# A later planned landing for the second chunk's queries and keys, and the clock-holding tile filled first

## The chip, the cores and the metric

The kernel runs on one core of a Trainium2 chip. The metric is the device time of one execution in microseconds (us), and lower is better. Ratios below 1 mean that a kernel is faster than the kernel before. A difference counts as faster or slower from 2%; below that it is "the same", although the repeated runs here resolve about 0.2%.

## The reference

```python
# q, k, v: [4, 8, 768, 64]
scores = q @ k.T / sqrt(64)
keep = causal                                    # heads 0, 2, 6
keep = causal & (first 4 keys | last 64 keys)    # the other heads
a = softmax(where(keep, scores, -1e9)) @ v
x = a.transpose(0, 2, 1, 3).reshape(3072, 512)   # tokens x (head, dim)
g, val = x @ w_gate, x @ w_val                   # d_ff = 1536
out = x + sigmoid(x @ w_res) * ((gelu(g) * val) @ w_out)
```

All inputs and the output are float32; the kernel computes in fp16 and accumulates in float32.

## The kernel before

The 3072 tokens are worked off in six chunks of 512. The kernel is written as a list of tasks. Each has an engine, a planned duration, a priority and the tasks that it depends on. A list scheduler runs when the program is built, and fixes the order of instructions on each engine; semaphores are then derived from the dependencies. So a planned duration or a planned landing changes nothing on the chip by itself. It changes the order, and an engine then waits in that order for whatever really comes late.

```python
# in the scheduler: when a load is planned to have landed
if t.dma:
    ...
    t.end = dma_free[e] + 1.6 + t.late
...
# the task g0 is the first gate matmul: with it the "warm" matmuls end
if t.name == "g0" and warming:
    warming = False
    cand["pe"] = [w for w in cand["pe"] if w.name != "warm"]
...
t_blank = G.add("dve", 0.1, lambda e: e.memset(blank[:, :], 0.0), [], -99, name="blank")
t_ident = G.add("dve", 0.1, lambda e: e.memset(ident[:, :], 0.0), [], -98, name="ident")
t_ident = G.add("pool", 0.3, aff(ident[:, :], ALU.not_equal, 1.0, ...), [t_ident], -58.5, name="const")
...                                        # m_causal, m_win: on GpSimd as well
# in loads_rows (chunks 0 and 1): queries and keys by rows, in halves for chunk 0
for j, src in enumerate((q, k)):
    t = dma("pool", base + 4 * gi + j, (h1 - h0) * n * 0.089, ..., bufs=[st])
...                                        # transposed on TensorE against ident (L676)
# fillers for TensorE, at the lowest priority
for _ in range(360):
    G.add("pe", 0.06, lambda e, warm=warm: e.matmul(at(warm)[:, 0:128], lhsT=blank[:, :], rhs=blank[:, :], ...),
          [t_blank], 1e9, bufs=[warm], name="warm")
load_weights()      # gate and value weights in three parts each, in turn: gate 1, value 1, gate 2, ...
```

GpSimd issues all loads of the inputs, which convert float32 to fp16, and it makes the identity (`ident`) and the masks in between. The warm matmuls are meant to hold TensorE's clock up until real work fills it. The string HINTS holds hand-found priorities of some hundred tasks, as "number of the task: priority".

The softmax here doesn't subtract the row's maximum and nothing guards it: scores larger than these inputs give would overflow.

Of the kernel before, what the change touches and what calls it, by code (L numbers as in the profile page):

```python
# [43 lines left out]


HINTS = (
    "0:598.78 2:-98.96 3:-24.27 16:511.03 398:-226.32 399:-81.95 400:-169.98 401:-133.18 406:592.76 "
    "428:669.65 590:-107.97 595:554.03 604:-62.97 609:119.02 611:508 631:-103.87 632:500.02 635:591.25 "
    "640:113.91 642:197.51 643:485.34 648:497.6 649:608.77 687:-2618.72 693:998.98 695:-156.54 696:-101.5 "
    "699:-194.37 703:460.62 704:468.99 706:91.16 707:1.21 708:-184.02 711:-2906.86 712:108.67 715:-113.61 "  # L50
    "722:-93.98 726:593.8 732:539.67 737:-3080.99 740:2426.17 743:-43.63 744:44.98 750:-84.74 755:-61.77 "
    "756:-226.32 757:-68.07 758:-100.39 762:-75.67 767:1467.66 783:2538.51 789:1088.69 791:2362.89 "
    "794:489.79 834:-1953.13 885:2499.66 897:2409.44 903:1361.62 910:1573 915:1075.62 921:1094.44 "
    "927:1527.46 933:2646.2 934:3345.41 946:3583 960:3450.9 963:1467.39 982:1981.84 984:1548.12 1014:3374.09 "
    "1025:2486.39 1037:3491.83 1060:2046.57 1061:2453.27 1067:3409.97 1068:1990.02 1069:3494.45 1076:2552.54 "
    "1081:2446.96 1082:3477.51 1099:2162.67 1105:3505.94 1111:3490.47 1117:3067.67 1144:3026.33 1146:3134.85 "
    "1150:118.46 1155:3543.75 1198:3516.67 1304:980.83 1313:4066.75 1341:4517.9 1343:4508.61 1358:985.12 "
    "1363:4003.98 1364:4417.91 1375:5441.35 1388:4117.01 1418:5399.99 1424:4517.89 1429:3494.32 1435:5479.84 "
    "1436:5423.25 1563:5565.33 1567:6542.91 1598:5535.71 1608:2079.98 1609:4991.07 1610:5503.31 1622:2043.57 "
    "1623:5529.25 1628:5543.06 1629:5543.02 1635:6420.01 1659:7430.01 1672:7417.77 1684:7455.84 "  # L60
)

class Task:
# [380 lines left out]
def c_mm(n, k=1):  # L444
    return k * max(0.029, n / 2400 + 0.0025)


def c_act(n):
    return 0.19 + n * 0.000834


def c_dve(n, rate=1.0, psum=True):
    return (0.125 if psum else 0.065) + n * 0.00104 / rate
# [6 lines left out]
def build_kernel(nc, q, k, v, w_gate, w_val, w_out, w_res, out):  # L460
    assert N_SINK <= 64 and WINDOW == 64
    G = Graph(nc)
# [16 lines left out]
    P_vk = Pool(many("vk", 2, [128, 8, DHEAD + 1], FP16))  # L479
# [21 lines left out]
    def at(buf):  # L501
        if buf.pool is P_ps:
            return psum[:, buf.slot[0] * 512:(buf.slot[-1] + 1) * 512]
        return buf.pool.items[buf.slot]

    def at16(buf):
        return at(buf).bitcast(FP16)
# [17 lines left out]
    t_blank = G.add("dve", 0.1, lambda e: e.memset(blank[:, :], 0.0), [], -99, name="blank")  # L525
# [17 lines left out]
    t_win = t_win0 + [spread(("dve",), 600, m_win[:, 5:7, :], m_win[:, 1:2, :].to_broadcast([128, 2, 128]), 256, t_win),  # L543
                      spread(("dve",), 600, m_win[:, 0, :], m_win[:, 1, :], 128, t_win)]
    for i, vk in enumerate(P_vk.items):
        P_vk.last[i] = [G.add("dve", 0.3, (lambda vk=vk: lambda e: e.memset(vk[:, :, :], 0.0))(), [], -94, name="vzero")]
    for i, va in enumerate(P_v.items):
        P_v.last[i] = [G.add("dve", 0.15, (lambda va=va: lambda e: e.memset(va[:, :, :, DHEAD:DHEAD + 1], 1.0))(),
                             [], -95, name="vones")]

    def dma(eng, prio, cost, out_ap, in_ap, bufs=(), deps=(), name="ld", grp=None):
        issue = 0.85 if eng == "pool" else 1.2
        return G.add(eng, issue, lambda e: e.dma_start(out_ap(), in_ap), deps, prio, bufs=bufs, dma=cost, name=name, grp=grp)  # L553
# [24 lines left out]
    def batch(b):  # L578
        if b not in batches:
            B_ = B()  # L580
            B_.v, B_.vs, B_.vk, B_.qkt = Buf(P_v), Buf(P_vs), Buf(P_vk), Buf(P_qkt)
            B_.vtok, B_.vstok, B_.qtok, B_.ktok = {}, {}, {}, {}

            B_.q6, B_.q6tok = None, {}
            batches[b] = B_
        return batches[b]
# [59 lines left out]
    def loads_rows(c, si, b, a, z):  # L646

        n = z - a
        BB = batch(b)
        st = Buf(P_st)  # L650
        lo, hi = a * 128, z * 128
        base = {0: -60, 1: -15, 2: 50}[c]
        groups = ((0, 4), (4, 8)) if c == 0 else ((0, 8),)
        tok = {}

        def sv(j, h0, h1, w):
            return at(st)[:, :].rearrange("p (j h w) -> p j h w", j=2, h=NHEAD)[:, j, h0:h1, 0:w]
        for gi, (h0, h1) in enumerate(groups):
            for j, src in enumerate((q, k)):
                t = dma("pool", base + 4 * gi + j, (h1 - h0) * n * 0.089,  # L660
                        (lambda j=j, h0=h0, h1=h1: lambda: sv(j, h0, h1, n * 64))(),
                        src[b, h0:h1, lo:hi, :].rearrange("h (p j) d -> p h (j d)", j=n), bufs=[st])
                for h in range(h0, h1):
                    tok[j, h] = t
        values(b, a, z, base + (10 if c == 0 else 2), False, c == 0)

        per = 1 if c == 0 or n == 4 else 2
        for k_ in range(0, NPAIR, per):
            ps_ = ORDER[k_:k_ + per]
            pr = 1000 * c - 492 + ps_[0] if c else 40 * k_ - 205  # L670
            for js in (((1,), (0,)) if c == 0 else ((0, 1),)):
                scr = Buf(P_ps, "scr" if c else "scr0")
                items = [(p, jj) for jj in js for p in ps_]

                def tr(e, items=items, scr=scr):
                    return [e.transpose(out=at16(scr)[64 * x:64 * x + 64, (m * n + i) * 128:(m * n + i + 1) * 128],  # L676
                                        in_=at(st)[:, (jj * NHEAD + h) * 256 + i * 64:(jj * NHEAD + h) * 256 + (i + 1) * 64],
                                        identity=ident[:, :])
                            for m, (p, jj) in enumerate(items) for i in range(n) for x, h in enumerate(PAIRS[p])]
                tt = G.add("pe", c_mm(128, n) * len(items), tr, [t_ident] + [tok[jj, h] for p, jj in items for h in PAIRS[p]],  # L680
                           pr, bufs=[st, scr], name="qkT")
                tt.mode = "col"


                def ev(on, p0=ps_[0], scr=scr, j0=js[0], m=len(items)):
                    def fn(e):
                        o = at(BB.qkt)[:, :, :, lo:hi].rearrange("c j (y x) w -> c x (j y) w", x=2)[:, p0 % 2]
                        m0 = j0 * 2 + p0 // 2
                        o = o[:, m0:m0 + m, :].rearrange("c m (p j) -> c m p j", j=n)
                        i_ = at16(scr)[:, 0:m * n * 128].rearrange("c (m j p) -> c m p j", m=m, j=n)  # L690
                        return e.tensor_copy(out=o, in_=i_) if on == "dve" else e.activation(out=o, in_=i_, func=AF.Copy)
                    return fn
                w = n * 128 * len(items)
                t = G.flex({"dve": (c_dve(w), ev("dve")), "act": (c_act(w), ev("act"))}, [tt], pr,
                           bufs=[scr, BB.qkt], name="qkE")
                for p, jj in items:
                    for i in range(a, z):
                        (BB.ktok if jj else BB.qtok)[p, i] = t
# [525 lines left out]
def bass_duo_attention_split__then__geglu_gated_residual_kernel(  # L1224
    nc: bass.Bass,
    q: bass.AP,
    k: bass.AP,
    v: bass.AP,
    is_retrieval: bass.AP,
    n_sink: bass.AP,  # L1230
    window: bass.AP,
    moe_w_gate: bass.AP,
    moe_w_val: bass.AP,
    moe_w_out: bass.AP,
    moe_w_res: bass.AP,
    out: bass.AP,
):
    assert int(n_sink) == N_SINK and int(window) == WINDOW
    build_kernel(nc, q, k, v, moe_w_gate, moe_w_val, moe_w_out, moe_w_res, out)
# [33 lines left out]
```

## Time and profile before

| | before |
|---|---|
| time, three runs | 272.18 us median, 271.61 to 272.54 |
| profiled execution | 272.37 us, of which the profile's span is 270.6 |
| idle TensorE ahead of the first warm matmul | 2.63 us |
| idle TensorE ahead of the second chunk's transposes | 0.53 us |
| TensorE after 36.78 us | without a gap, to 267.66 us |
| after the last matmul | 2.9 us (270.6 less 267.66) |

The prediction below shows the lines on which this rests. Three more views of the kernel before are needed. The first is GpSimd's timeline: start and duration in us, engine, line, operation.

```profile
1.32 0.88 POOL L553 DMA_DIRECT2D qks<-in_q_dram  x1 [0.81 <-DVE ident L526]
2.29 0.30 POOL L511 TENSOR_SCALAR_AFFINE_SELECT ident<-ident 128x128 f16<-128x128 f16 x1
2.53 0.77 POOL L553 DMA_DIRECT2D qks<-in_k_dram  x1
```

GpSimd issues the first q load, makes the identity, and only then issues the first k load. The second view is the list of DMA issues for the first 4 us: tile, queue, count, KB of each, us from issue to landing.

```profile
qks<-in_k_dram POOLq DMA_DIRECT2D x1, 256.0 KB, 5.4
```

Issued at 2.53, that k load landed at 7.93. The third view is TensorE's timeline, where the first q and then the first k transposes are.

```profile
6.05 1.06 PE L676 MATMUL ps<-ident,qks 128*64 128x128 f16 x16
...
7.99 0.64 PE L676 MATMUL ps<-ident,qks 128*64 128x128 f16 x16
```

The k transposes start right after the k load has landed.

### The profile page before, as it was taken

Reading aid. Unit: us, or ns where it says so; the run is one execution under the profiler, and the core shown is the slowest. Engines: PE = TensorE matmul, PEld = TensorE weight load, DVE = VectorE, ACT = ScalarE, POOL = GpSimd, SP = SyncE. Lnnn points to the kernel's source line nnn. Section 1 sums busy time; section 2 is a strip of 40 time slices with the busy share of each in tenths; the row PEclk is TensorE's granted clock in tenths of the full one; section 3 lists DMA queues with packets and bytes.
Section 4 is the critical chain, followed back from the end, with each engine's and each line's share of the span. In section 5 each row is a group of like instructions: output and inputs, shape, how many; then the busy total and the mean of one; then the engine's idle time right before and its main releaser. Section 6 shows DMA issues by size and latency. Waiting matters only on the chain.

```text
span 270.6 us, 5686 instructions
## 1 busy us (share of the span) xinstructions
PE 264.4 (98%) x2392; PEld 139.0 (51%) x2392; DVE 141.3 (52%) x275; ACT 139.6 (52%) x215; POOL 87.0 (32%) x124
## 2 busy tenths in 40 slices
PE   6999999999999999999999999999999999999995
PEld 5778554465444456444455444455444455444444
DVE  1798236387444466534477533376444377434344
ACT  2785456864245877233784233776323778043300
POOL 8999409995743037993000000000000000000000
PEclk9999999999999999999999999999999999999999
DMA  6999999999999999999964100013100014100013
GB/s 82 172 203 207 185 179 229 170 160 172 176 183 151 154 126 221 183 174 162 174 125 119 39 0 0 2 41 85 74 0 0 0 41 80 61 20 0 0 39 119
DMA packets 96506, 29.12 MB, mean 108 GB/s; under 512 B 84448, under 2 KB 92896, under 8 KB 96480
## 3 DMA queue, kind: packets, MB, share of 16 engines
q0 software_dynamic: 70320, 14.69, 64.3%
q1 hardware_dynamic: 26160, 14.07, 27.9%
q8 instruction: 19, 0.31, 0.5%
q14 instruction: 7, 0.06, 0.1%
HBM read 29.36 MB, written 6.29 MB: 132 GB/s over the span
## 4 chain that ended last, share of the span: by engine, by line
PE 85%; DMA 7%; POOL 6%; issue 1%; DVE 1%; POOLq 0%; DVEq 0%
PE ps L1111 41%; PE ps L1156 23%; PE ps L1141 8%; DMA qks<-in_k_dram 7%; PE ps L852 4%; PE ps L986 3%; POOL qks L553 2%; PE ps L976 2%; PE ps L1000 1%; PE ps L1065 1%; POOL va L553 1%; POOL wv L553 1%; PE ps L676 1%; PE ps L943 1%; POOL wg L553 1%
## 5 line engine op out<-in xcount | busy, mean ns | idle before, releaser
L1123 ACT ACTIVATE gact<-ps 128x512 f16<-128x512 f32 x68 | 40.2, 597 | 73.3 <-PE ps L1111 71.9
L1125 DVE SCALAR_TENSOR_TENSOR hT<-gact,ps 128x512 f16<-128x512 f16 x68 | 45.7, 687 | 61.7 <-ACT gact L1123 34.0
L1111 PE MATMUL ps<-xT,wv 128*128 128x512 f16 x272 | 74.6, 379 | 0.0
L1111 PE MATMUL ps<-xT,wg 128*128 128x512 f16 x272 | 74.1, 379 | 0.0
L1156 PE MATMUL ps<-wo,hT 128*128 128x512 f16 (+2 forms) x312 | 70.7, 363 | 0.0
L1111 PEld LDWEIGHTS ps<-xT,wv 128*128 128x128 f16 x272 | 26.3, 98 | 31.3 <-DMA wv<-in_moe_w_val_dram 0.4
L1111 PEld LDWEIGHTS ps<-xT,wg 128*128 128x128 f16 x272 | 26.3, 98 | 30.5 <-ACT xT L1072 0.6
L1156 PEld LDWEIGHTS ps<-wo,hT 128*128 128x128 f16 x312 | 27.2, 98 | 26.2 <-issue 1.0
L553 POOL DMA_DIRECT2D qks<-in_k_dram x36 | 28.6, 834 | 32.9 <-DMA qkt<-qks 22.5
L868 ACT ACTIVATE er<-ps 128x1024 f16<-128x1024 f32 (+4 forms) x40 | 34.2, 890 | 7.9 <-PE ps L852 7.6
L553 POOL DMA_DIRECT2D qks<-in_q_dram x36 | 28.8, 846 | 0.8 <-DVE ident L526 0.8
L1160 DVE SCALAR_TENSOR_TENSOR otile<-srs,ps 128x512 f32<-128x512 f32 (+2 forms) x26 | 16.8, 644 | 17.4 <-PE ps L1156 17.2
L1141 PE MATMUL ps<-wr,xT 128*128 128x512 f16 x96 | 24.5, 380 | 0.0
L553 POOL DMA_DIRECT2D va<-in_v_dram x24 | 21.5, 944 | 3.0 <-PE ps L1000 3.0
L1144 ACT ACTIVATE srs<-ps 128x512 f32<-128x512 f32 x24 | 14.3, 597 | 13.6 <-PE ps L1141 13.6
L852 PE MATMUL ps<-qkt 64*128 64x64 f16 (+3 forms) x391 | 17.2, 213 | 0.1
L1163 DVE TENSOR_TENSOR otile<-otile,xtok 128x512 f32<-128x512 f32 (+2 forms) x26 | 16.8, 647 | 0.7
L1043 DVE TENSOR_TENSOR xtok<-ps,rcp 128x512 f32<-128x512 f32 (+1 forms) x28 | 16.9, 609 | 0.5
L852 PEld LDWEIGHTS ps<-qkt 64*128 64x128 f16 x391 | 9.9, 94 | 9.3 <-issue 4.9
L868 ACT ACTIVATE es<-ps 128x1024 f16<-128x1024 f32 (+1 forms) x14 | 12.6, 900 | 3.0 <-PE ps L852 3.0
L1141 PEld LDWEIGHTS ps<-wr,xT 128*128 128x128 f16 x96 | 8.5, 98 | 9.5 <-issue 0.6
L1173 PE MATMUL ps<-blank 128*128 128x128 f16 x109 | 10.8, 248 | 2.6 <-DVE blank L525 2.6
(69 smaller groups left out, 216.1 us busy)
## 6 DMA issues: line engine op xcount, KB each, us to landing
out_dram<-otile SPq DMA_DIRECT2D x23, 256.0 KB, 2.0
va<-in_v_dram POOLq DMA_DIRECT2D x24, 128.0 KB, 18.5
qks<-in_k_dram POOLq DMA_DIRECT2D x32, 64.0 KB, 12.4
qks<-in_q_dram POOLq DMA_DIRECT2D x32, 64.0 KB, 13.0
wg<-in_moe_w_gate_dram POOLq DMA_DIRECT2D x3, 512.0 KB, 11.5
wv<-in_moe_w_val_dram POOLq DMA_DIRECT2D x3, 512.0 KB, 11.9
wo<-in_moe_w_out_dram POOLq DMA_DIRECT2D x4, 384.0 KB, 23.7
vs<-va SPq DMA_DIRECT2D x4, 260.0 KB, 6.7
```

The costliest lines, as they stand in the source:

```text
L553: return G.add(eng, issue, lambda e: e.dma_start(out_ap(), in_ap), deps, prio, bufs=bufs, dma=cost, name=name, grp=grp)
L852: return [e.matmul(at(scr)[:, oo:oo + w], lhsT=side(BB, low, 1)[half, k0:k0 + 128], rhs=side(BB, low, 0)[half, qq:qq + w], start=True, sto ...
L868: return e.activation(out=o, in_=i_, func=AF.Exp, scale=SM_SCALE)
L1043: t2 = G.add("dve", c_dve(2 * n * 64), lambda e: e.tensor_tensor(out=xview(), in0=avv(0, DHEAD), in1=scale(), op=ALU.mult), [t1] + xdeps, ...
L1111: return lambda e: [e.matmul(at(dst)[:, :], lhsT=w[:, ci, f * 128:(f + 1) * 128], rhs=at(xtbuf)[:, ci, :], start=(ci == 0), stop=(ci == NC ...
L1123: ta = G.add("act", c_act(512), (lambda gb=gb, ga=ga: lambda e: e.activation(out=at(ga)[:, :], in_=at(gb)[:, :], func=AF.Gelu))(), [tg], p ...
L1125: th = G.add("dve", c_dve(512), (lambda vb=vb, ga=ga, f=f: lambda e: e.scalar_tensor_tensor(out=at(h)[:, f, :], in0=at(ga)[:, :], scalar=0 ...
L1141: e.matmul(at(rb)[:, :], lhsT=at(xtbuf)[:, ci, s], rhs=wr[:, ci, :], start=(ci == 0), stop=(ci == NCB - 1))
L1144: ta = G.add("act", c_act(512), (lambda rb=rb, sr=sr: lambda e: e.activation(out=at(sr)[:, :], in_=at(rb)[:, :], func=AF.Tanh, scale=0.5)) ...
L1156: e.matmul(at(fb)[:, w], lhsT=at(h)[:, fi, s], rhs=wo[:, fi, w], start=(fi == 0), stop=(fi == NF - 1))
L1160: t1 = G.add("dve", c_dve(n), (lambda fb=fb, sr=sr, ot=ot, w=w: lambda e: e.scalar_tensor_tensor(out=at(ot)[:, w], in0=at(sr)[:, w], scala ...
L1163: t2 = G.add("dve", c_dve(n), (lambda ot=ot, lt=lt, w=w: lambda e: e.tensor_tensor(out=at(ot)[:, w], in0=at(ot)[:, w], in1=at(xbuf)[:, lt, ...
```

## The change

The intent has two parts. The loads of the second chunk's queries and keys are planned to land 1.2 us later, nearer to when they do land, so that the scheduler puts other work ahead of their transposes. And the other fills on VectorE are made to depend on the blank tile, so that it is filled first and the clock-holding matmuls start sooner. The hints were searched anew for this plan.

```diff
 HINTS = (
-    "0:598.78 2:-98.96 3:-24.27 16:511.03 398:-226.32 399:-81.95 400:-169.98 401:-133.18 406:592.76 "
     (13 more lines removed)
+    "1:-142.02 3:-32.5 13:-14.98 398:-205.14 399:-3161.01 400:-242.48 401:-60.67 406:194.11 430:523.84 "
     (12 more lines added)
 )
@@
     for i, vk in enumerate(P_vk.items):
-        P_vk.last[i] = [G.add("dve", 0.3, (lambda vk=vk: lambda e: e.memset(vk[:, :, :], 0.0))(), [], -94, name="vzero")]
+        P_vk.last[i] = [G.add("dve", 0.5, (lambda vk=vk: lambda e: e.memset(vk[:, :, :], 0.0))(), [t_blank], -94, name="vzero")]
     for i, va in enumerate(P_v.items):
         P_v.last[i] = [G.add("dve", 0.15, (lambda va=va: lambda e: e.memset(va[:, :, :, DHEAD:DHEAD + 1], 1.0))(),
-                             [], -95, name="vones")]
+                             [t_blank], -95, name="vones")]
@@ in loads_rows
                         src[b, h0:h1, lo:hi, :].rearrange("h (p j) d -> p h (j d)", j=n), bufs=[st])
+                t.late = 1.2 if c else 0.0
                 for h in range(h0, h1):
                     tok[j, h] = t
```

Task 2 is the making of the identity on GpSimd. Its hint of -98.96 is gone, which is how the first k load came ahead of it.

## The prediction

> **What bounds the kernel now.** I read the page first, for the busy shares and the chain that ended last.
>
> ```profile
> PE 264.4 (98%) x2392; PEld 139.0 (51%) x2392; DVE 141.3 (52%) x275; ACT 139.6 (52%) x215; POOL 87.0 (32%) x124
> ...
> PE 85%; DMA 7%; POOL 6%; issue 1%; DVE 1%; POOLq 0%; DVEq 0%
> ```
>
> TensorE is busy 98% of the span and carries 85% of the chain. DMA and GpSimd carry 13%, so I asked for the chain in order of time, to see where those 13% lie.
>
> ```profile
> 15.33 0.74 POOL wv L553
> 16.07 2.56 POOL qks L553 x3
> 18.63 18.01 DMA qks<-in_k_dram
> 36.64 0.14 issue
> 36.78 0.64 PE ps L676 x16
> 37.42 1.83 PE ps L1111 x8
> ```
>
> All of it comes before 36.78 us: GpSimd issues loads one behind the other, and the last of the second chunk's queries and keys, issued at 18.63, lands 18.01 us later. From there on the chain is TensorE alone, until the output's tail. The timeline of TensorE has only two idle stretches that it names in the whole run:
>
> ```profile
> 2.63 3.49 PE L1173 MATMUL ps<-blank 128*128 128x128 f16 x31 [2.63 <-DVE blank L525]
> ...
> 36.78 0.64 PE L676 MATMUL ps<-ident,qks 128*64 128x128 f16 x16 [0.53 <-DMA qks<-in_k_dram]
> ```
>
> The numbers are start, duration and, in brackets, the idle time before. The first is the wait of the clock-holding ("warm") matmuls for their blank tile, the second the wait of the second chunk's transposes for that load. Asking for three stretches confirms it (columns: stretch, its length, busy time, clock, DMA share, GB/s):
>
> ```profile
> 20.60:36.25 15.65, 15.64 (x133) 1.00 1.61 190
> 36.25:36.78 0.53, 0.00 (x1) 1.00 2.43 155
> 36.78:266.40 229.62, 229.62 (x1923) 1.00 0.86 98
> ```
>
> From the first gate/value matmul (20.60) to the last matmul, 0.53 us are idle out of 245.8. After that come 4.2 us of last evictions and output.
>
> **What the Trainium skill says.** "TensorE: Matmul & The Clock Gate", section "What's actually happening", has the array at half clock until it has been busy for about 3.4 us, and says that this varies from run to run. The trace agrees roughly: the 31 first warm matmuls take 3.4 us from 2.63 (110 ns each), those at 8.56 take 0.73 us for ten. The same page, "Back-to-back issue gap", puts a warm 512-column matmul at 512/2.4 + 2.5 = 216 ns; here a pair takes 0.43 us (35.21 to 35.65). "DMA: Bandwidth & Descriptors", "Issuing engines are not separate DMA queues", says that all loads share the same 16 engines. The trace agrees: with up to about 190 GB/s flowing, later issues take longer and longer from issue to landing (4.3 us for the first q load, 18.0 us for the load above).
>
> **The change, part by part.** The real work is untouched. The counts of every TensorE instruction but the warm ones are the same in both orders; warm ones go from 109 to 116, all ahead of the first gate/value matmul. What the diff changes are the planned landing, the priorities and two fills on VectorE, and hence the order on every engine.
>
> *The blank tile.* VectorE now runs ident, blank, then the four other fills. Before, blank came last:
>
> ```profile
> 0.89 0.11 DVE L526 MEMSET ident<- 128x64 uint32 x1 [0.89 <-PEq L1255]
> 1.12 0.10 DVE L548 MEMSET va<- 128x48 f16 x1
> 1.25 1.04 DVE L546 MEMSET vk<- 128x520 f16 x2
> 2.42 0.10 DVE L548 MEMSET va<- 128x48 f16 x1
> 2.46 0.11 DVE L525 MEMSET blank<- 128x64 uint32 x1
> ```
>
> Blank will be ready at about 1.2, so warm matmuls start about 1.4 us earlier (2.63 to 1.25), now 42 in the first run. At 110 ns for 4.0 us (2.63 to about 6.65, where the transposes speed up) that is 37 slow ones and five fast: the end is at about 5.6 instead of 6.05. The transposes behind them wait for the first q load, which lands at 1.34 + 4.3 = 5.64, so they may start 0.3 to 0.4 us earlier. But the next transposes wait for keys: issued 2.53, landing 5.4 later, at 7.93, and the trace shows them starting at 7.99. That gate isn't moved. The blank part is worth 0 at the end.
>
> *The second chunk's transposes.* Before, the first one asked for is of the segment whose keys land last (18.63 + 18.01 = 36.64). In the new order more real work stands ahead of the transposes: counting columns streamed from the first gate/value matmul, 35,547 before and 39,269 after, so (39,269 - 35,547)/2400 = 1.55 us more, at 2.4 columns per ns. TensorE will reach them at 37 to 38 us and not wait. The 0.53 us go.
>
> *What the new order wants earlier.* To have that work, it takes later weights sooner. Weight landings, each issue start plus its time to landing: gate 1 18.1, value 1 20.7, gate 2 23.2, value 2 25.7, gate 3 28.3, value 3 30.8. Going through the new order against these, with 1.013 times the ideal streaming time (15.65 us less about 0.5 for small matmuls against 14.81 ideal):
> - First half's attention should be finished a little sooner, as VectorE now runs the second big vs copy (0.69) and one xT copy (0.29) after its last normalisation and not before. The first gate matmuls go at about 20.0 to 20.4, and then value matmuls wait for value 1 until 20.75, where before there was work that needed none. At 20.75 both orders have done equal real work: 21,946 columns plus 0.15 us before, 21,296 + 1,024 after, 9.29 and 9.30 us.
> - The next 4.41 ideal us, with the same 0.5 overhead, bring it to 25.66 at the first full-width gate matmul (before: 25.64). 2.14 more bring it to 27.8 at its first use of gate 3, which lands at 28.3. A new wait of about 0.5 us. Before, gate 3 was first used at 28.67.
> - From 28.35, 9.38 ideal us lead to the second chunk's transposes at 37.85. Before, the same amount of real work stood at: 36.78 plus the difference of (16.36 + 8.87) - (14.81 + 9.14) = 1.28 ideal, 1.29 at this rate, 38.07. The new kernel leads by 0.22 us.
>
> The sum: -0.53 for the wait taken away, +0.5 for gate 3, -0.2 for real work in place of warm work and waits earlier, that is -0.2. GpSimd also issues the first k load before making ident (some 0.3 us earlier), which could bring the whole stream of loads 0 to 0.3 us forward, and with it the gate-3 wait. I take 0.1 of it: -0.3 in all.
>
> *Later.* After 38 us TensorE does the same matmuls in another order. Changes between tile shapes after the first gate/value matmul go from 86 to 88, worth nothing that can be seen. The third chunk's loads start when the second chunk's transposes free their buffer, at about 41.1 instead of 40.64; its last transposing DMA was issued at about 74 and takes 7 us, its first use is at 87, so 6 us of slack absorb that. The first output weights (45.7 to 51.5) are used from about 47. The last 20 rows of TensorE's order, with the split last tile, are alike.
>
> **The rivals.** (1) The whole 1.4 us of the blank tile come through, or both waits do: 272.18 - 1.4 - 0.53 = 270.3. For it: they are the two idle stretches that TensorE shows. Against it: the keys' landing at 7.93 and the weights at 20.7 and 28.3 stand between. (2) The wait for queries and keys is gone and nothing takes its place: -0.53 or, with the 0.2 of earlier real work, -0.7, 271.5. For it: gate 3 misses by only 0.5 us. Against it: a slower start would use that up, but costs as much itself. (3) The new order makes ScalarE or VectorE late somewhere in the six attention stages, and TensorE meets new waits: the priorities of about a hundred tasks are new, and before there is not one idle stretch after 36.78 to hide behind. One or two such waits of 0.5 us would make it 272.5 to 273. Against it: ScalarE and VectorE are only 52% busy, and the plan has the same rules.
>
> **Range and chances.** 272.18 - 0.3 = 271.9. Three runs of before spread over 0.9 us, rival 1 lies 1.6 below and rival 3 about 1 above, so 270.8 to 273.0. 2% is 5.4 us; the startup as a whole offers less than 2 us and nothing seen costs 5, so within 2% gets 0.975.
>
> **What would show it.** Right: warm matmuls starting near 1.25; the second run of transposes still near 7.95; no wait for in_k_dram near 37; a new wait of 0.3 to 0.6 us for wg near 28.3, and maybe one for wv near 20.5; no idle stretch over 0.2 after 38; tail 4.2 us. Wrong: the second transposes moving by as much as the blank, landings moved by a microsecond, or TensorE idling on ScalarE or VectorE later.

## The result, and the profile after

| | before | after |
|---|---|---|
| time | 271.89 us median of 4 (271.56 to 272.54) | 271.17 us median of 4 (270.81 to 271.22) |
| ratio | | 0.9968, 95% interval 0.9945 to 0.9991 |
| span of the profile | 270.6 us | 269.3 us |

Ratios are computed as the mean time of one kernel's fast runs over that of the other's of the same rounds, so they are not quite the ratio of the medians that are quoted. The changed kernel is 0.3% faster, which is within 2%.

The page of the changed kernel gives busy shares and the shares of the chain that ended last.

```profile
PE 264.8 (98%) x2399; PEld 139.2 (52%) x2399; DVE 142.5 (53%) x275; ACT 138.8 (52%) x215; POOL 87.3 (32%) x124
...
PE 93%; DMA 3%; POOL 1%; DVE 1%; issue 0%; POOLq 0%; DVEq 0%
```

TensorE carries 93% of the chain, where it was 85%. The chain in order of time shows what most of the 3% of DMA is.

```profile
6.28 7.03 DMA va<-in_v_dram
13.35 0.33 PE ps L986 x5
```

The chain now leaves the loads at 13.35 us, with a value load, and not at 36.64 with the second chunk's keys. TensorE's timeline has the stretches that the prediction asked for.

```profile
1.14 4.33 PE L1173 MATMUL ps<-blank 128*128 128x128 f16 x42 [1.14 <-DVE blank L524]
5.64 0.64 PE L676 MATMUL ps<-ident,qks 128*64 128x128 f16 x16 [0.17 <-DMA qks<-in_q_dram]
...
7.04 0.64 PE L676 MATMUL ps<-ident,qks 128*64 128x128 f16 x16
...
13.35 0.33 PE L986 MATMUL ps<-va,er 128*128 128x65 f16 x5 [0.33 <-DMA va<-in_v_dram]
...
36.85 1.08 PE L676 MATMUL ps<-ident,qks 128*64 128x128 f16 x32
```

The warm matmuls start at 1.14 (2.63 before). The q transposes start at 5.64 and run at full speed. The k transposes start at 7.04, 0.95 us earlier than before. The second chunk's transposes are no longer preceded by a wait, and start at nearly the same moment as before (36.78), although 1.3 us more real work lies ahead of them. In return there is a new wait of 0.33 us for a value load. The stretches from the first gate or value matmul (columns: stretch, its length, then for each engine its busy time and count; clock, DMA share and GB/s last) confirm that nothing else is idle.

```profile
19.45:36.85 17.40, 17.40 (x153) 11.28 (x149) 9.03 (x27) 8.53 (x19) 11.20 (x14) 1.00 1.62 190
36.85:265.20 228.35, 228.35 (x1918) 112.66 (x1918) 120.04 (x206) 118.20 (x173) 58.02 (x76) 1.00 0.84 98
```

The view of the weight loads into TensorE shows the predicted wait for gate 3:

```profile
27.22 0.55 PEld L1111 LDWEIGHTS ps<-xT,wg 128*128 128x128 f16 x4 [0.27 <-DMA wg<-in_moe_w_gate_dram]
```

It is there, but TensorE itself was held for some 0.15 us only: the four matmuls before it started at 26.63, four of their kind take 0.44 us, and it started at 27.22 and not at 27.07. VectorE has the order that was planned, with blank second:

```profile
0.89 0.11 DVE L525 MEMSET ident<- 128x64 uint32 x1 [0.89 <-PEq L1255]
0.97 0.11 DVE L524 MEMSET blank<- 128x64 uint32 x1
```

And GpSimd has its first k load ahead of the identity.

```profile
2.19 0.76 POOL L552 DMA_DIRECT2D qks<-in_k_dram  x1
3.02 0.32 POOL L510 TENSOR_SCALAR_AFFINE_SELECT ident<-ident 128x128 f16<-128x128 f16 x1
```

In the view of the DMA issues of these first 4 us, it takes 4.7 us to land, not 5.4. (Landings here are the start of an issue plus this rounded time, good to 0.05 us.)

```profile
qks<-in_k_dram POOLq DMA_DIRECT2D x1, 256.0 KB, 4.7
```

Issued 0.34 us sooner and 0.7 us faster, the first keys land at 6.89 instead of 7.93. And it is not this load alone: gate 1 lands at 17.04 (18.14 before), value 1 at 19.51 (20.71), gate 3 at 27.18 (28.27), the last of the second chunk's keys at 35.50 (36.67). The whole stream is 1.0 to 1.2 us earlier. The prediction had taken those landings as fixed.

The order of instructions after the second chunk's transposes costs nothing and saves nothing. From their start to the end of the last matmul it is 267.66 - 36.78 = 230.88 us before and 266.44 - 36.85 = 229.59 after. The difference, 1.29 us, is the real work moved ahead of the transposes. In both profiles TensorE has no idle stretch from there on. So the span's gain of 1.3 us was made before 37 us.

### The profile page after: what moved, and what is told of

Its sections match the earlier page's. It is cut to its first block, busy times and chain, and to the rows that moved or that the text cites. A ratio compares the mean times of both kernels' runs of the same rounds, so it can differ in the third digit from the quotient of the medians.

```text
span 269.3 us, 5699 instructions
## 1 busy us (share of the span) xinstructions
PE 264.8 (98%) x2399; PEld 139.2 (52%) x2399; DVE 142.5 (53%) x275; ACT 138.8 (52%) x215; POOL 87.3 (32%) x124
## 4 chain that ended last, share of the span: by engine, by line
PE 93%; DMA 3%; POOL 1%; DVE 1%; issue 0%; POOLq 0%; DVEq 0%
PE ps L1111 44%; PE ps L1156 23%; PE ps L1141 8%; PE ps L852 5%; PE ps L986 3%; DMA va<-in_v_dram 3%; PE ps L1093 3%; PE ps L976 2%; PE ps L1000 2%; PE ps L1065 2%; POOL qks L552 1%; PE ps L943 1%; PE ps L676 1%; PE ps L1173 1%; DVE otile L1163 0%; DVE otile L1160 0%
## 5 line engine op out<-in xcount | busy, mean ns | idle before, releaser
L852 PE MATMUL ps<-qkt 64*128 64x64 f16 (+4 forms) x391 | 16.9, 213 | 0.0
L1072 ACT ACTIVATE xT<-ps 128x512 f16<-128x512 f16 (+1 forms) x13 | 6.2, 498 | 12.4 <-PE ps L1065 12.4
```

The lines of the kernel that those rows point to most:

```text
L852: return [e.matmul(at(scr)[:, oo:oo + w], lhsT=side(BB, low, 1)[half, k0:k0 + 128], rhs=side(BB, low, 0)[half, qq:qq + w], start=True, sto ...
```

## The experiments

The theories are these. **Start** (the expectations may shorten a theory to a letter): all the gain is made ahead of the second chunk's transposes, through loads or TensorE's first work coming earlier, and the new order by itself is worth nothing. Within it, either the k load ahead of the identity does it, or the early blank tile, or it is chance, because the loads of the profile before were late in that one execution. **Order**: the transposes put later, and so the keys' wait taken away, are what gains.

The experiment kernels move single tasks after the scheduler has run, and derive positions, dependencies and semaphores again from the lists. A helper does this; an edit `("pool", 391, 2)` takes task 391 out of GpSimd's list and puts it in again ahead of task 2.

```python
def reorder(G, moves=(), more=0, fewer=0):       # more, fewer: warm matmuls at the head of TensorE's list
    for eng, seq, where in moves:
        p = G.prog[eng]
        t = next(x for x in p if x.seq == seq)
        p.remove(t)
        p.insert(next(n for n, x in enumerate(p) if x.seq == where), t)
    ...                                          # then positions and a global order anew
```

In the names, b_ kernels start from the kernel before and a_ kernels from the changed one. All results were correct. The first table has the times; every batch has its own runs of the kernel before, 11 in each, with medians of 272.45 (first batch, 271.5 to 272.74), 271.59 (second, 270.98 to 272.4) and 271.78 us (third, 271.03 to 272.65).

| kernel | batch | median us (range) of n | ratio to before, 95% interval |
|---|---|---|---|
| b_again | 1 | 271.6, one run | not computed |
| b_pool | 1 | 271.56 (271.18 to 272.5) of 6 | 0.9979, 0.9960 to 0.9998 |
| b_blank | 1 | 271.49 (270.78 to 272.45) of 6 | 0.9976, 0.9953 to 0.9998 |
| b_both | 1 | 271.18 (270.87 to 271.46) of 6 | 0.9961, 0.9945 to 0.9977 |
| a_again | 2 | 271.14 (270.93 to 271.38) of 5 | 0.9983, 0.9968 to 0.9998 |
| a_pool | 2 | 271.44 (270.9 to 271.86) of 6 | 0.9989, 0.9973 to 1.0005 |
| a_blank | 2 | 272.04 (271.73 to 272.35) of 6 | 1.0016, 1.0001 to 1.0031 |
| b_late | 2 | 272.89 (272.11 to 273.89) of 6 | 1.0050, 1.0030 to 1.0069 |
| b_all | 3 | 271.12 (270.98 to 271.29) of 6 | 0.9970, 0.9952 to 0.9988 |
| a_both | 3 | 271.6 (271.41 to 273.12) of 6 | 0.9990, 0.9968 to 1.0011 |
| a_g3 | 3 | 271.08 (270.84 to 271.99) of 6 | 0.9972, 0.9951 to 0.9993 |
| a_g3va | 3 | 271.09 (270.83 to 271.33) of 6 | 0.9968, 0.9949 to 0.9986 |

The second table has what the profiled execution of each shows, in us from the start of its span. The k landing is worked out as the issue's start plus its time to landing.

| kernel | first k load lands | first gate or value matmul | second chunk's transposes start | last matmul ends |
|---|---|---|---|---|
| before | 7.93 | 20.60 | 36.78 | 267.66 |
| b_again | 6.93 | 20.45 | 35.97 | 266.86 |
| b_pool | 6.90 | 19.82 | 35.70 | 266.59 |
| b_blank | 6.93 | 20.34 | 35.87 | 266.75 |
| b_both | 6.90 | 20.04 | 35.70 | 266.59 |
| b_late | 7.72 | 20.40 | 37.84 | 268.16 |
| b_all | 6.90 | 19.77 | 36.16 | 266.49 |
| after | 6.89 | 19.45 | 36.85 | 266.44 |
| a_again | 6.90 | 19.20 | 36.75 | 266.35 |
| a_pool | 8.32 | 20.40 | 37.64 | 267.24 |
| a_blank | 6.89 | 19.57 | 37.33 | 266.92 |
| a_both | 8.23 | 20.36 | 38.23 | 267.82 |
| a_g3 | 6.99 | 19.20 | 36.68 | 266.27 |
| a_g3va | 6.89 | 19.49 | 37.05 | 266.65 |

Except in b_late and b_all, which move the transposes themselves, the last two columns differ by 230.88 or 230.89 in the old order and by 229.59 or 229.60 in the new one, whatever happened earlier. This is what makes the start of the transposes a good gauge for the rest of the run. To compare the orders by it, 1.29 is taken off in the new one.

### b_again: the kernel before, once more

There is no edit.

> The kernel before, unchanged, as a control for the landings. Theory A (the order of issue on GpSimd moved the loads): the first k load lands at 7.9, gate 1 at 18.1, the last keys of the second chunk at 36.7, each within 0.2 us, and TensorE waits about 0.5 us for those keys. Rival B (luck of the DMA engines from run to run): these landings differ from the first profile by 0.5 us or more.

The unchanged kernel showed another profile than the first time: a span of 269.8 and not 270.6 us. The view of the DMA issues of its first 4 us has the k load, and its TensorE timeline the two runs of transposes.

```profile
qks<-in_k_dram POOLq DMA_DIRECT2D x1, 256.0 KB, 4.4
```

```profile
7.88 0.64 PE L676 MATMUL ps<-ident,qks 128*64 128x128 f16 x16
...
35.97 0.64 PE L676 MATMUL ps<-ident,qks 128*64 128x128 f16 x16
```

The k load was issued at the same 2.53 us and landed 1.0 us earlier than in the first profile, and with it every later load: gate 3 at 27.26, the last second-chunk keys at 35.57. There was no wait for keys at all. So the 0.53 us, which the change was meant to take away and which the prediction counted, are not always there. The kernel before has an early and a late state of its load stream (the two of its profiles; more in the section on what the runs say together), and its first profile was of the late one. The k transposes start at 7.88 here, long after 6.93: they now stand behind the warm matmuls and the slow q transposes (6.05, 1.06 us long again), not behind the load.

### b_pool, b_blank, b_both: one part at a time, and two

```diff
 # b_pool: the first k load (391) ahead of the making of the identity (2)
+    reorder(G, moves=[("pool", 391, 2)])
 # b_blank: the blank tile's fill (0) second on VectorE; 42 instead of 31 warm matmuls at the start
+    reorder(G, moves=[("dve", 0, 17)], more=11)
 # b_both
+    reorder(G, moves=[("pool", 391, 2), ("dve", 0, 17)], more=11)
```

> The kernel before with one swap: GpSimd issues the first k load ahead of making ident. Theory A: k lands near 6.9, gate 1 near 17.0, the last keys near 35.6; the wait of 0.53 near 36.3 goes, and the time falls by 0.5 to 0.8 us. The k transposes stay near 7.9, as the late warm matmuls stand before them. Rivals B and C (C: the order of the fills on VectorE moved the loads): landings as before, time within 0.2 us of before.

> The kernel before with the blank fill second on VectorE and 11 more warm matmuls in the first run (42, as in the changed kernel), nothing else. Theory A, and my prediction: warm matmuls start near 1.2, k transposes still near 7.9 behind the load, 0.5 us of waiting near 36.3 stay, time within 0.2 us of before. Rival C: the loads land 1 us earlier and the time falls by 0.5 us or more.

> Both edits in the kernel before. Theory A: neither is worth it alone but together they let the k transposes start near 7.0, the first gate matmul near 19.7 and the landings stay 1 us early: 1.0 to 1.3 us off the time, all that the changed kernel has, without moving the second chunk's transposes (wait for them left: 0.2 to 0.4). If the new order of TensorE is what gives the gain: 0.3 us or less.

All three are faster than the kernel before in this batch, by 0.2 to 0.4%. b_blank was expected to stay within 0.2 us of before, and came out as fast as b_pool (0.9976 and 0.9979). But eight of the eleven runs of before in this batch lie above 272 us, and the medians of both kernels, 271.49 and 271.56, lie with its three others (271.5 to 271.72). So by timed runs alone the two parts can't be told apart, nor either of them from an early execution of before. With both parts in the old order the ratio is 0.9961, as good as the changed kernel's own (0.9968 and 0.9983). The swap on GpSimd brings the k load to 6.90. In TensorE's timeline of b_pool, the k transposes start earlier than expected, and a part of the wait for the second chunk's keys is back:

```profile
7.12 0.64 PE L719 MATMUL ps<-ident,qks 128*64 128x128 f16 x16
...
35.70 0.64 PE L719 MATMUL ps<-ident,qks 128*64 128x128 f16 x16 [0.28 <-DMA qks<-in_k_dram]
```

The k transposes were to stay near 7.9, behind the late warm matmuls. These did start at 2.63 again, but took 3.17 us and not 3.49, and the q transposes ran at full speed behind them (0.64). So the moment at which the clock rises moves the start about as much as the early blank does, and each profile is one draw of that too. In the old order TensorE is early enough here to meet the keys, which caps what a faster start can bring at 35.70, in b_pool and b_both alike. In the timed runs the early blank on top of the swap nevertheless gave 271.18 against 271.56 us, or 0.9961 against 0.9979. The intervals of the two overlap, and in the profiles the last matmul of both ends at 266.59.

In b_blank, with the identity still first, the k load landed at 6.93, as in b_again. In TensorE's timeline of b_blank, this is what the early blank tile then brings:

```profile
7.07 0.64 PE L719 MATMUL ps<-ident,qks 128*64 128x128 f16 x16
...
13.54 0.33 PE L1029 MATMUL ps<-va,er 128*128 128x65 f16 x5 [0.63 <-DMA va<-in_v_dram]
...
35.87 0.64 PE L719 MATMUL ps<-ident,qks 128*64 128x128 f16 x16
```

The k transposes start 0.81 us earlier than in b_again, but the second chunk's only 0.10 earlier. A wait for the second value load stands in between. That load took 7.2 us to land, and 5.8 in b_again, so these two executions differ in more than the blank tile.

### a_again, a_pool, a_blank: taking one part out of the changed kernel

```diff
 # a_pool: the identity (2) ahead of the first k load (391) again
+    reorder(G, moves=[("pool", 2, 391)])
 # a_blank: blank last on VectorE again, 31 warm matmuls; the other fills no longer depend on blank
+    for t in G.prog["dve"]:
+        if t.name in ("vones", "vzero"):
+            t.deps = []
+    reorder(G, moves=[("dve", 0, 413)], fewer=11)
```

> The changed kernel, unchanged. The runs so far say that the stream of loads has two states, whatever the kernel: early (first k load 6.9, gate 1 17.0, last keys 35.6) and late (1.0 to 1.1 us more each), and that the kernel before was profiled in the late one (272.5 against 271.6 us). Theory M (the state makes most of the measured gain): the changed kernel runs near 271.1 in the early state, 0.5 us under the early runs of before; a late run, if one comes, near 272.2 as predicted from a late trace. Rival (the change is worth 0.9 us by itself): all runs of before, early or late by their time, lie 0.9 above the changed kernel's of the same state.

> The changed kernel with one swap undone: GpSimd makes ident ahead of issuing the first k load, as before. If GpSimd's order decides the state of the stream: late runs (near 272.2) in half of the six or more. If the state is chance that neither order rules: as the changed kernel, within 0.2 us of it.

> The changed kernel with the blank fill last again and 31 warm matmuls first, as before. If the early warm matmuls matter once the loads are early: the q transposes start at 6.05 and the k transposes at 7.9 as in the control of before, the first gate matmul some 0.5 us later than 19.45, and the time is 0.3 to 0.6 us longer. If the loads gate it (my prediction: the blank part is worth 0): no more than 0.15 us.

a_again repeats the changed kernel without an edit, and repeats its result: 271.14 us, 0.9983. With the identity first again (a_pool), the profiled execution was one with late loads (k at 8.32) and the slowest of the six, 271.86 us; the others lay between 270.9 and 271.51. The three or more runs near 272.2 that were expected if GpSimd's order decides did not come. With the blank tile last again (a_blank) the whole gain is gone: 272.04 us, 0.90 more than a_again, and the intervals of the two ratios do not overlap. Why is not shown. TensorE's timeline of a_blank has a later start of the k transposes and a wait for gate 3.

```profile
6.06 0.64 PE L722 MATMUL ps<-ident,qks 128*64 128x128 f16 x16
...
7.46 0.64 PE L722 MATMUL ps<-ident,qks 128*64 128x128 f16 x16
...
27.70 1.04 PE L1157 MATMUL ps<-xT,wg 128*128 128x512 f16 x4 [0.29 <-DMA wg<-in_moe_w_gate_dram]
```

The k transposes start at 7.46, against 7.06 in a_again, although the keys had landed at 6.89 in both. But this is not what set the time of this execution. The chains of a_blank and then of a_again, in order of time, both go back to the load of gate 3:

```profile
14.71 12.94 DMA wg<-in_moe_w_gate_dram
```

```profile
14.61 12.46 DMA wg<-in_moe_w_gate_dram
```

It landed at 27.65 and at 27.07, and the transposes start 9.63 us after its first use in both (27.70 to 37.33, 27.12 to 36.75). So the 0.58 us between the two starts is this load, issued 0.10 later and 0.48 slower; an earlier start would have waited for it. The last keys landed alike, at 35.4. The rest of the difference of the two profiled executions (271.74 and 270.93 us) is a longer tail: 3.1 us after the last matmul, against 2.9. The tail is 2.9 us in all profiles but those of a_blank and a_both (3.5). Whether a late blank tile leads to either in the new order, or chance does, these runs don't show, and five of the six timed runs have no profile.

### b_late: only the later transposes, by hand

```diff
 # before, the first 16 of the second chunk's transposes (442) moved behind eight 512-column matmuls
+    reorder(G, moves=[("pe", 442, 430)])
```

> The kernel before with one edit on TensorE: the second chunk's first transposes go behind the eight 512-column matmuls that followed them. If the wait for those keys is a cost of the late state alone: late runs fall from 272.5 to 272.0, early runs stay at 271.6, and no run waits for the keys. If reordering in itself helps: early runs fall too.

It failed as an experiment. I had put all 64 transposes in a row, and TensorE's timeline shows them waiting for each other's buffers.

```profile
39.60 0.64 PE L719 MATMUL ps<-ident,qks 128*64 128x128 f16 x16 [0.67 <-ACT qkt L734]
40.58 0.64 PE L719 MATMUL ps<-ident,qks 128*64 128x128 f16 x16 [0.34 <-ACT gact L1166]
```

The waits of 0.67 and 0.34 us are for ScalarE, which empties the PSUM tiles. They are a new cost of the experiment (272.89 us) and say nothing of the change, whose scheduler spread the transposes out.

### b_all and a_both: everything but the new order, and the new order alone

```diff
 # b_all: before, with k first, blank second, 42 warm, and the first 16 transposes behind four matmuls
+    reorder(G, moves=[("pool", 391, 2), ("dve", 0, 17), ("pe", 442, 731)], more=11)
 # a_both: after, with the identity first, blank last (as in a_blank), 31 warm
+    reorder(G, moves=[("pool", 2, 391), ("dve", 0, 413)], fewer=11)
```

> The kernel before with the early k issue, the early blank (42 warm matmuls first), and the second chunk's first transposes moved behind four 512-column matmuls: the three parts of the change by hand, in the old order of everything else. From the second chunk's transposes to TensorE's last matmul every profiled run of the old order took 230.89 us. Theory S (only the start counts, the rest of the new order is worth nothing): no wait for keys is left, the start lies where it does in the changed kernel (35.5 to 35.6, counted at the old place of the transposes), and the time equals the changed kernel's within 0.2 us, 0.1 to 0.3 under the kernel with the first two parts. Rival (the new order is itself worth something): at least 0.3 us slower than the changed kernel, measured as ratios to before.

> The changed kernel with ident made before the k load, blank last and 31 warm matmuls first: the new order with the whole old start. Theory S: slower than the changed kernel by 0.7 to 1.0 us and no faster than before, ratio 1.000 to 1.003, as the new order wants gate 3 earlier and waits for it 0.2 to 0.5 us. Rival: the new order alone keeps half of the gain or more, ratio 0.998 or lower.

b_all keeps the old order of everything else and reaches 271.12 us (0.9970), the changed kernel's time. TensorE's timeline has no idle stretch that it names after the warm start's. a_both has the new order without the new start, and its ratio is 0.9990, an interval that holds 1. Its profiled execution was a late one and the slowest of six (273.12 us), and it shows what the new order does when the loads are late.

```profile
8.23 0.64 PE L722 MATMUL ps<-ident,qks 128*64 128x128 f16 x16 [0.84 <-DMA qks<-in_k_dram]
...
28.60 1.04 PE L1157 MATMUL ps<-xT,wg 128*128 128x512 f16 x4 [0.27 <-DMA wg<-in_moe_w_gate_dram]
```

Gate 3 landed at 28.59, even later than in the first profile of the kernel before (28.27). The new order swaps the wait for the keys for one on gate 3, just as predicted. The start theory holds: the old order with the new start gains all of it (b_both, b_all). The new order alone gains nothing that can be resolved, although its interval, from 0.9968 to 1.0011, is too wide to exclude a gain. One thing fits no theory here: a_blank, with the keys first, is no faster than a_both, with the identity first (272.04 and 271.6 us, ratios 1.0016 and 0.9990 in different batches, intervals overlapping).

### a_g3 and a_g3va: the two new waits taken away

```diff
 # a_g3: after, the first use of gate 3 moved a few tasks later
+    reorder(G, moves=[("pe", 761, 743)])
 # a_g3va: the same, and the second value load issued ahead of a mask's select on GpSimd
+    reorder(G, moves=[("pe", 761, 743), ("pool", 395, 6)])
```

> The changed kernel with one matmul task (two of 512 columns, the first that reads gate 3) moved behind four tasks that don't read it. If the wait for gate 3 sets the start in the changed kernel (0.15 us in its profile, transposes always 9.6 us after it): no wait near 27, and 0.1 to 0.3 us faster. If ScalarE or VectorE set the pace there: the wait comes back elsewhere and the time stays.

> The same with the second value load issued one operation earlier on GpSimd, as TensorE waits for it in two profiles (0.33 us at 13.35). If its landing follows its issue: another 0.1 to 0.3 us off. If the stream sets the landing: nothing more.

The two are at 271.08 and 271.09 us, against 271.17 and 271.14 of the changed kernel in other batches: nothing that these runs resolve. The second value load, issued at 5.90, landed at 12.00 and not at 13.28, without any gain in time (in b_again, issued at 6.27, it landed at about 12.1 as well, so not all of this is the move's). So of 0.15 and 0.33 us of waiting nothing comes through; a gain of 0.15 alone could not be resolved. In the profile of a_g3va TensorE names no idle stretch after its first warm matmul at 1.13: the 42 warm matmuls took 4.66 us and the q transposes 1.06, so the clock rose late, and TensorE's own work set the pace. For the other runs this was not shown. No kernel of the study beats the changed one beyond the spread.

### What the runs say together

The first k load landed at 6.89 to 6.99 us in all eight profiles in which it was issued ahead of the identity. With the identity first, it landed at 6.93 in two profiles and at 7.72 to 8.32 in four. If the order made no difference, a split as uneven as this, none of eight late and four of six, would come up in 15 of 1001 draws (an estimate that takes the 14 profiles as alike in all else). The timed runs of the kernels before and after fit this. Of the kernel before there are 37 in all; 18 lie above 272 us, with a mean of 272.42, and 19 below, with a mean of 271.48. Only three of the 37 lie between 271.9 and 272.3. The share above 272 differs: 2 of 4 in the first rounds, then 8, 3 and 5 of 11. Two further executions of it were profiled, so that their landings are known, and they lie on the right sides (272.37 late, 271.6 early). Of the 39 timed runs of kernels with k first, leaving out a_blank, one lies above 272 (a run of b_pool, 272.5). But three of the six of a_blank do, whose keys landed early, and of the 18 of b_blank, a_pool and a_both, with the identity first, only three do, none of them of a_pool, whose profile was a late one at 271.86. So the line at 272 sorts the kernel before and no other, and that the swap pins the early state rests on the profiles. The nine runs of the changed kernel have a mean of 271.12. From this I estimate that it gains 271.48 - 271.12 = 0.36 us over an early execution of before and 272.42 - 271.12 = 1.30 over a late one; half and half that is some 0.8, against the 0.87 measured in the first rounds (means of 271.97 and 271.10). The traces say the same: the transposes started, in terms of the old order, at 36.85 - 1.29 = 35.56, 0.41 ahead of the early profile of before (35.97) and 1.22 ahead of the late one (36.78).

Sorting timed runs at 272 us is a reading of their spread, as those runs have no profiles. Why the k load is sometimes a microsecond late when GpSimd makes the identity between two issues was not shown, either. From 4 to 6 us, the loads flow alike in the late profile of before and in b_again (192 and 195 GB/s); from 6 to 7 the late one has 162 and the early one 187. But b_late's profile, late as well, has 191 there, so the rate alone isn't it.

## Why the prediction was right or wrong

**The class and the range were right.** 271.17 us lies within 270.8 to 273.0 and within 2%. It was predicted at 271.9, a gain of 0.3, where the medians differ by 0.72.

**Right in mechanism.** Predicted and seen: warm matmuls from about 1.25 (1.14); their end at about 5.6 (5.47); q transposes 0.3 to 0.4 us earlier (0.41, limited by the q load's landing); no wait for keys near 37; a new wait for gate 3; 1.29 us of real work moved ahead (1.29); the tail unchanged (2.9 us after the last matmul in both, not the 4.2 that the prediction gave: it counted from 266.40, and TensorE works until 267.66); no new idle stretch after 38 us, so that rival 3 did not come about. Rival 2, 271.5 without a wait in place of the old one, came nearer than the main line, but for another reason than it gave. The end of the warm matmuls was met partly by luck. The prediction let the clock rise at 6.65, but all 16 q transposes of before ran slow, from 6.05 to 7.04 (1.06 us; 0.64 when fast), and the same 42 warm matmuls took between 3.80 and 4.66 us in other profiles. And the growing times to landing, which the prediction reads as agreeing with shared DMA engines, are those of loads from one issuing engine, so they do not test that.

**The step that failed** is "That gate isn't moved." The gate was the k load's landing at 7.93. It moved to 6.89, and the k transposes went at 7.04. The prediction had noticed that GpSimd issues the k load ahead of the identity, had allowed "0 to 0.3 us" for it and taken 0.1; the landings in the changed profile were 1.0 to 1.2 us earlier. That is the mis-sized term. Its root is that one trace's landings were taken as the kernel's. b_again shows the same landing at 6.93 in the unchanged program, so most of the difference between the two first profiles, 0.8 of the 1.2 us at the end of the last matmul (267.66, 266.86 and 266.44), is the state that the profile before happened to be in. The swap pins the early state in every profile taken; that is a gain on average, and not in the best case.

**Following from it**, the working went wrong by one constant. Gate 3's first use was put at 28.35 and came at 27.22, 1.13 earlier; from there to the transposes it was predicted 9.5 us (37.85 - 28.35) and measured 9.63. (The prediction's factor of 1.013 is a slip: (15.65 - 0.5)/14.81 is 1.023, which makes 9.60 of its 9.38 ideal us.) So the path after gate 3 was right and everything ahead of it was late by the stream's shift. The gate-3 wait was 0.15 and not 0.5, since work and load moved together. In a late execution of the new order (a_both), it was 0.27. The wait for value 1 at 20.75 did not appear: its first use was at 19.89, with the weights landed at 19.51.

**Whether the blank tile is worth 0 is open.** By timed runs it is not: a_blank loses 0.90 us against a_again in one batch, and b_both gains 0.38 on b_pool, though these intervals overlap. In the profiles it came to 0.1 us or nothing: the last matmul ends at 266.86 in b_again and 266.75 in b_blank, both with early keys, and at 266.59 in b_pool and b_both; what a_blank's profile loses lies in the landing of gate 3 and in the tail. With the identity first, leaving the blank tile late shows no loss by ratio (a_both 0.9990, a_pool 0.9989, in different batches), though the mean times, 271.91 and 271.40 us, are 0.5 apart through two runs of a_both over 272.

**The new waits' worth** was overrated too: taking both away in a_g3va brought at most 0.1 us, not resolved.

## What to carry to other kernels

Landings read from one trace are one draw: profile the unchanged kernel a second time before you count a DMA wait of half a microsecond as a gain, and look for two clusters in its times. Gates in a row (here warm-up, keys, value and weight loads) must be judged together: a start that is 0.8 us earlier can be worth 0.1 at the end when the next load stands in the way. When an order found by a search is faster, try its few changes in the first microseconds in the old order before crediting the order itself.

## What the Trainium skill lacked or had wrong

- "DMA: Bandwidth & Descriptors", section "Anatomy of one DMA — SWDGE (gpsimd) path", gives a fit of 2.0 us plus the bytes over 436e3. For 256 KB (262,144 bytes) that makes an estimate of 2.6 us. The very first q load, with no other load in flight ahead of it, took 4.3 us from issue to landing (issued at 1.32, landed at 5.6, in every profile), so the fit is too low for a first converting load of this kernel. (256 KB is what it writes, in fp16; with the 512 KB of float32 that it reads the estimate is 3.2.) Under a full stream a load of the same size took 18.0 us, as the prediction shows.
- No page tells that the load stream of one unchanged program can start in two states, about 1 us apart, from one execution to the next: the first k load landed at 6.93 or at 7.72 to 8.32 us with one GpSimd operation between the first two issues, and at 6.89 to 6.99 in eight profiles without it.
- "TensorE: Matmul & The Clock Gate", section "What's actually happening", is confirmed in that the moment at which the clock rises varies: the same first 42 warm matmuls took 3.80 to 4.66 us in the profiles of this study. The ±500 ns that it gives for this is too narrow here. In b_both their pace goes from 107 to 56 ns after 26 of them, 2.7 us after the first; in a_g3va all 42 and the q transposes behind them ran slow, for over 5 us. It is another reason why single profiles differ by some tenths of a microsecond at the start.
